# Four output products open at the end, V of the first unit moved, and two rates of a layout clock, in a kernel of two attentions

## The chip, the core and the metric

The kernel runs on one core of a Trainium2 chip. The metric is the time of one execution on the device in microseconds (us), as the median of several runs. The profile is of one execution, taken by the hardware profiler; the last digit of the times of its single instructions is 10 ns.

## What is computed

Two attention layers with their own inputs, both with 2048 positions, width 1024 and 32 heads of 32. Layer A looks back over 8 positions in steps of 2, layer B over 256 positions in a row; their results are put side by side.

```python
qkv = (x @ wqkv).reshape(B, S, 3, H, Dh).transpose(2, 0, 3, 1, 4)
q, k, v = qkv
# A: keys at pos - 2*i for i in 0..7, masked where negative
# B: keys at pos - i for i in 0..255, masked where negative
p = softmax(where(mask, (q @ k.T) * Dh ** -0.5, -1e9))
o = (p @ v).transpose(0, 2, 1, 3).reshape(B, S, D) @ wo
out = concatenate([A, B], axis=-1)
```

## The kernel before

**Units and groups.** The work is cut into eight units of 512 positions (`UNITS`, line 833): units 0 to 3 are layer B (called dense here: scores of up to 384 columns), units 4 to 7 layer A, whose even and odd positions are taken apart so that its window is 8 neighbours (scores of 136 columns). Each unit has eight groups of four heads. With 64 groups in all, group 8u + s is group s of unit u.

**Three-part products.** Each operand of the big products is split into a high part (a cast to fp32r) and a low part (the original less the high part). A product is then three matmuls per step of 128 (`TERMS`: high by high, high by low, low by high). Making the parts is the work of `Stream.parts` (line 126): the cast is done by VectorE (DVE, L129), the subtraction by DVE (L137) or GpSimd (POOL, L134), whichever the layout clock holds to be free earlier. A weight of 128 x 1024 gives one w tile (three buffers); a piece of x gives two x tiles of half its size (ten buffers, `NX`). Raw pieces arrive by DMA in three buffers, so the load of item i + 3 can only start when item i has been split. The first eight loads are issued by ScalarE (ACT), all later ones by POOL (L103).

**Per unit.** For each group: q and k (L363, 24 matmuls of 512 columns each), copied out by ACT (L314) and DVE (L318) and restacked by DMAs that SyncE (SP) issues (L328). V comes in four parts of two groups each (L415, 256 columns), after the q and k of the groups that `V_SLOTS` names. The four parts of the previous unit's attention output are multiplied by `wo` (L455) in eight output products, placed by `O_SLOTS`. Each of these is a chain of eight steps, one for each group, so its last step needs the last group's output.

**Attention of one group.** Sixteen first scores (L614) go to banks of the score ring (four PSUM banks); DVE takes their row maximum with the mask (L619), ACT exponentiates and sums (L624). When all sixteen are done: a logarithm (L637), three small DVE instructions (L642 to L645), a transpose on PE (L653), a copy by DVE (L657) and a DMA back into the q tile (L660). Only then can the second scores run (L509 for the window, L696 for dense), whose exponentials (L514, L701) are masked by DVE or POOL (L524, L520, L682, L685) and multiplied by V (L548, L741). The group's output is copied out in a high part by ACT (L577) and a low part by DVE (L581).

**What sets the order.** Nothing is scheduled by the chip beyond each engine's own queue. While it builds the program, the kernel keeps a layout clock (`Clock`, line 33): it holds estimated times at which each engine and queue becomes free. A loop (line 803) picks from four lists (row transposes, second scores, first scores, big products) the item whose estimated ready time is earliest and emits it; follow-up work on other engines is emitted when the clock passes its time. So a changed rate in the clock alters no instruction but can alter the order of all of them, and which engine does a split or a mask. The clock doesn't model the single output buffer (`NST = 1`): `copy_out` (line 377) chooses between ACT and DVE by when they are free.

**The end.** The eight products of the last unit follow everything else. `TAIL = 2` of them run their first seven steps before the last group's output is there (lines 789 to 797), in two of the three accumulator banks of the big products. Each finished product is copied to the output buffer (L379 by ACT or L382 by DVE) and stored by a DMA that ACT issues (L470).

Of the kernel before, what the change touches and what calls it, by code (L numbers as in the profile page):

```python
# [14 lines left out]
P = 128  # L15
NG = 8
NK = 8
# [6 lines left out]
VPARTS = ((0,2),(2,2),(4,2),(6,2))  # L24
V_SLOTS = {0: 0, 1: 1, 5: 2, 7: 3}
O_SLOTS = {2: (0, 1), 3: (2, 3), 4: (4, 5), 5: (6, 7)}
NX, NST = 10, 1
TAIL, LAND, XAT = 2, 0.45, 1
C1, C3, CG, CV = 0.114, 0.2, 0.231, 0.243
TERMS = ((0, 0), (0, 1), (1, 0))  # L30

# [1 line left out]
class Clock:  # L33
# [26 lines left out]

    def fetch(self, dur, *ready):

        t = max(self.use("pool", 1.0, *ready) + 0.6, self.free["loads"])
        self.free["loads"] = t + dur + 0.5 * max(0.0, min(2 * dur, self.free["copies"] - t))
        return self.free["loads"] + LAND

# [20 lines left out]
class Stream:  # L87
# [19 lines left out]
    def split_to(self, n):  # L107
        while self.split < min(n, len(self.items)):
            i = self.split
            self.load_to(i + 1)  # L110
            raw, t0 = self.raw.pop(i)
            if self.items[i][0] == "x":
                self.tiles[i], self.ready[i] = [], []
                for h in range(2):
                    t = self.xpool.tile([P, 2, S], F32R, tag="x", name="x")
                    self.ready[i].append(self.parts(t, raw[:, h * S:(h + 1) * S], t0))
                    self.tiles[i].append(t)
            else:
                t = self.wpool.tile([P, 2, 1024], F32R, tag="w", name="w")
                self.ready[i] = self.parts(t, raw, t0)  # L120
                self.tiles[i] = t
            self.split += 1
            end = self.ready[i] if self.items[i][0] != "x" else max(self.ready[i])
            self.ck.defer(end, lambda n=i + NRAW + 1: self.load_to(n))

    def parts(self, t, raw, t0):
# [20 lines left out]
def kernel(ctx, tc, xs, wqk, wv, wo, outs, units):  # L147


    nc = tc.nc  # L150
    U = len(units)
# [15 lines left out]
    ck = Clock()  # L167


    plan = []  # L170
    for u in range(U):
        for s in range(NG):
            if u and s in O_SLOTS:
                plan += [("o", u - 1, n) for n in O_SLOTS[s]]
            plan.append(("qk", u, s))
            if s in V_SLOTS:
                plan.append(("v", u, V_SLOTS[s]))
        if u + 1 < U:
            plan.append(("x", u + 1))
    plan += [("o", U - 1, n) for n in range(NG)]  # L180
    items, where = [], {}

    def item(key, kind, ap):
        where[key] = len(items)
        items.append((kind, ap))

    def unit_x(u, *gs):
        for g in gs or range(4):
            item(("x", u, g), "x", xs[u][:, 2 * g:2 * g + 2, :])
# [5 lines left out]
    for p in plan:  # L195
        ly = units[p[1]][0]
        if p[0] == "o":
            item(p, "w", wo[ly, p[2]])
        elif p[0] == "v":
            s0, n = VPARTS[p[2]]  # L200
            for g in range(n):
                if n == 2:
                    item(p + (g,), "w", wv[ly, s0 + g])
                else:
                    w4 = wv[ly, s0 + g // 2:s0 + g // 2 + 3:2, :, g % 2 * 512:g % 2 * 512 + 512]
                    item(p + (g,), "w", w4.rearrange("t p c -> p t c"))
        elif p[0] == "qk":
            for t in range(2):
                if p + (t,) not in where:
                    item(p + (t,), "w", wqk[ly, 2 * p[2] + t])  # L210
        else:
            if NG - 1 in V_SLOTS:
                item(("qk", p[1], 0, 0), "w", wqk[units[p[1]][0], 0])
                unit_x(p[1])
            else:
                unit_x(p[1], 0)
                item(("qk", p[1], 0, 0), "w", wqk[units[p[1]][0], 0])
                unit_x(p[1], 1, 2, 3)
    st = Stream(nc, ck, raws, wpool, xpool, items)
# [42 lines left out]
    xt, xready, ot = {}, {}, {}  # L262
    done, waiting = {}, {}
# [22 lines left out]
    rg, rs, ro = Ring(psg, 7 - NS, "g"), Ring(pss, NS, "s"), Ring(pso, 1, "o")  # L286
# [7 lines left out]
    def latest(*ts):  # L294
        return None if any(t is None for t in ts) else max(ts)
# [81 lines left out]
    def copy_out(dst, ps, bank, ring):  # L377
        if max(ck.free["act"], ck.now) + 0.48 <= max(ck.free["dve"], ck.now) + 0.6:
            nc.scalar.copy(dst, ps)  # L379
            e = ck.use("act", 0.48, ck.now + ck.SEM)  # L380
        else:
            nc.vector.tensor_copy(dst, ps)  # L382
            e = ck.use("dve", 0.6, ck.now + ck.SEM)
        ring.give(bank, e)
        return e
# [52 lines left out]
    def o_items(u, n):  # L438
        h = {}

        def ready(k):
            if (u * NG + k) not in done["ot"]:
                return None
            if k == 0:
                st.split_to(where["o", u, n] + 1)
                h["r"] = st.ready[where["o", u, n]]
                return latest(rg.when(), h["r"], done["ot"][u * NG])
            return done["ot"][u * NG + k]

        def run(k):  # L450
            if k == 0:
                h["ps"], h["b"] = rg.take()
                h["w"], _ = st.get(where["o", u, n])
            for i, (a, b) in enumerate(TERMS):
                nc.tensor.matmul(h["ps"], h["w"][:, a, k * P:(k + 1) * P], ot[u, k][:, b, :],  # L455
                                 start=(k == 0 and i == 0), stop=(k == NK - 1 and i == 2))
            if k == 3 and (u < U - 1 or n != TAIL - 1):
                st.split_to(where["o", u, n] + 2)

        def after(k):  # L460
            if k == NK - 1:
                done["out"][u, n] = True
                for f in list(stores.values()):
                    f()
                o = stp.tile([P, S], F32, tag="ost", name="ost")
                e = copy_out(o, h["ps"], h["b"], rg)

                def store():
                    if stores.pop((u, n), None):
                        nc.scalar.dma_start(outs[u, n], o)  # L470
                        ck.load(0.8, e)

                stores[u, n] = store
                ck.defer(e, store)

        return [(lambda k=k: ready(k), lambda k=k: run(k), 3 * CG, lambda k=k: after(k)) for k in range(NK)]

    def x_items(u):
# [110 lines left out]
    def attention(u, s):  # L589
# [5 lines left out]
        v = vbuf[vp]  # L595
        h = {"left": 16, "rows": None}
        one, two = [], []

        def first(b, j):
            if "nm" not in h:  # L600
                h["nm"] = small.tile([P, 16], F32, tag="nm", name="nm")
                h["sm"] = small.tile([P, 16], F32, tag="sm", name="sm")
            if dense:
                full, mask = 384, cst["mask_d"]
                cut = 0 if has_halo else max(0, 256 - P * b)
            else:
                full, mask = 136, cst["mask_w"]
                cut = 8 if (b == 0 and not has_halo) else 0
            n = full - cut
            c1 = 256 + P * b + P  # L610
            c0 = c1 - n
            i = j * 4 + b
            ps, bank = rs.take()
            nc.tensor.matmul(ps[:, :n], q[0:96, j, b * P:(b + 1) * P], kk[0:96, j, c0:c1],  # L614
                             start=True, stop=True)
            nm, sm = h["nm"][:, i:i + 1], h["sm"][:, i:i + 1]

            def top():
                nc.vector.tensor_tensor_reduce(ps[:, :n], ps[:, :n], mask[:, cut:full], scale=-1.0, scalar=BIG,  # L619
                                               op0=ALU.add, op1=ALU.min, accum_out=nm)  # L620
                e = ck.use("dve", (n + 80) / 960, ck.now)

                def total():
                    nc.scalar.activation(ps[:, :n], ps[:, :n], AF.Exp, bias=nm, scale=-1.0, accum_out=sm)  # L624
                    e2 = ck.use("act", (n + 61) / 1200 + 0.19, e)
                    rs.give(bank, e2)
                    h["left"] -= 1
                    if h["left"] == 0:
                        ck.defer(e2, log_sum)

                ck.defer(e - 0.1, total)

            return top
# [131 lines left out]
    for u in range(U):  # L765
        for s in range(NG):
            a, b = attention(u, s)
# [21 lines left out]
    n = TAIL  # L789
# [13 lines left out]
    while True:  # L803
# [3 lines left out]
        for name, seq in seqs.items():  # L807
# [3 lines left out]
            t = seq[pos[name]].ready()  # L811
# [4 lines left out]
        if ck.later and (best is None or ck.later[0][0] < best[0]):  # L816
            t = ck.later[0][0]
# [3 lines left out]
        t, name = best  # L821
# [52 lines left out]
```

## Time and profile before

| | us |
|---|---|
| median of 3 runs | 1974.42 |
| lowest and highest | 1971.13, 1975.38 |
| the profiled execution | 1973.82 |
| its span, first to last instruction | 1972.1 |
| PE without work, in all, first matmul's 8.05 included | 43.9 |
| mean granted PE clock | 0.987 |

A busy PE is not PE at its peak: matmuls are pipelined, and a run of them is priced by the distance from start to start. Lines of the timeline give start, length, engine, line, operation, output and input tiles, count, and in brackets the idle time of the engine ahead of it with what ended it. Lines of a table of stretches give the stretch, its length, the busy time of PE, PEld (weight loads), DVE, ACT and POOL with instruction counts, then the granted PE clock, the DMA share and GB/s. A line of waits gives who waited for what, the total, how often, and the longest.

### The profile page before, as it was taken

The page shows a single profiled execution, that of the slowest core. Times are in us where ns is not written, and L with a number is a line of the kernel's source. Part 1 is how long each engine was busy: PE and PEld are TensorE (multiplying, and loading weights), DVE is VectorE, ACT ScalarE, POOL GpSimd, SP SyncE. Part 2 cuts the span into 40 slices and gives each one's busy share as a digit, 9 for nine tenths or more (in the row PEclk, how much of TensorE's full clock was granted, in tenths as well). Part 3 has the DMA queues.
Part 4 walks back from the last instruction along what each step waited for, and adds up shares of the span by engine and source line. Part 5 has one row for each costly group of instructions (what it writes and reads, how often), then busy time and mean ns, then how long its engine had stood idle before and what let it go on. Part 6 is the DMA issues. An engine that isn't in the chain of part 4 may idle for free.

```text
span 1972.1 us, 36479 instructions
## 1 busy us (share of the span) xinstructions
PE 1924.7 (98%) x12608; PEld 1619.8 (82%) x12608; DVE 1295.7 (66%) x3762; ACT 957.5 (49%) x3137; POOL 708.7 (36%) x923
## 2 busy tenths in 40 slices
PE   7999999999999999999999999999999999999998
PEld 6878887888877878788878888978888788888886
DVE  5687776678665786567865657655666557666653
ACT  3565554475654656555563344423534334434441
POOL 4334343444433434443443323233332333233221
PEclk9999999999999999999999999999989999999998
DMA  5555546455546465345645647455553565556442
GB/s 176 150 139 153 160 124 178 132 153 157 152 136 174 121 189 149 117 140 148 177 119 146 173 139 196 128 149 170 149 163 116 174 177 162 141 146 172 136 126 75
DMA packets 136502, 294.92 MB, mean 150 GB/s; under 512 B 14464, under 2 KB 42112, under 8 KB 136320
## 3 DMA queue, kind: packets, MB, share of 16 engines
q1 hardware_dynamic: 85632, 124.82, 26.1%
q0 software_dynamic: 40320, 146.82, 22.9%
q10 hardware_dynamic: 10368, 20.98, 2.9%
q8 instruction: 100, 1.64, 0.4%
q14 instruction: 82, 0.67, 0.1%
HBM read 163.58 MB, written 27.26 MB: 97 GB/s over the span
## 4 chain that ended last, share of the span: by engine, by line
PE 84%; DVE 7%; DMA 6%; ACT 2%; issue 1%; SPq 0%; POOL 0%; DVEq 0%; ACTq 0%; POOLq 0%
PE g L363 31%; PE g L455 16%; PE g L415 16%; PE s L614 7%; PE s L696 5%; PE o L741 4%; PE s L509 3%; DMA qst<-rt 3%; PE o L548 2%; DMA kst<-nat 1%; DMA raw<-xs 1%; DVE x L137 1%; DVE w L129 1%; ACT s L624 1%; DVE w L137 1%
## 5 line engine op out<-in xcount | busy, mean ns | idle before, releaser
L363 PE MATMUL g<-x,w 128*128 128x512 f32 x3072 | 801.9, 401 | 8.6 <-DVE w L129 8.0
L134 POOL TENSOR_TENSOR w<-raw,w 128x512 fp32r<-128x512 f32 x225 | 392.5, 1745 | 897.2 <-PE s L614 285.7
L363 PEld LDWEIGHTS g<-x,w 128*128 128x128 f32 x3072 | 562.0, 191 | 110.9 <-DVE w L129 8.4
L624 ACT ACTIVATE s<-s,nm 128x384 f32<-128x384 f32 (+3 forms) x1024 | 452.3, 443 | 231.0 <-DVE nm L619 227.1
L415 PE MATMUL g<-w,x 128*128 128x256 f32 x3072 | 413.3, 285 | 0.0
L415 PEld LDWEIGHTS g<-w,x 128*128 128x128 f32 x3072 | 392.7, 191 | 1.9 <-issue 0.6
L455 PE MATMUL g<-ot,w 128*128 128x512 f32 x1536 | 384.2, 397 | 3.6 <-DVE w L129 2.9
L455 PEld LDWEIGHTS g<-ot,w 128*128 128x128 f32 x1536 | 283.8, 190 | 58.1 <-DVE w L129 3.6
L619 DVE CUSTOM_DVE_ANT_0 s<-s,mask_d 128x384 f32<-128x384 f32 (+2 forms) x512 | 262.0, 556 | 72.9 <-PE s L614 71.5
L614 PE MATMUL s<-kst,qst 96*128 96x384 f32 (+3 forms) x1024 | 238.7, 303 | 16.2 <-ACT s L624 7.1
L701 ACT ACTIVATE pbuf<-s 128x384 f32<-128x384 f32 (+2 forms) x480 | 197.1, 507 | 85.5 <-PE s L696 81.8
L614 PEld LDWEIGHTS s<-kst,qst 96*128 96x128 f32 x1024 | 181.3, 192 | 60.5 <-ACT s L624 18.1
L624 ACT ACTIVATION_READ_ACCUMULATOR s<-s,nm 128x1 f32 x1024 | 210.2, 205 | 0.0
L619 DVE CUSTOM_DVE_ANT_0 s<-s,mask_w 128x136 f32<-128x136 f32 (+1 forms) x512 | 142.4, 322 | 98.4 <-PE s L614 96.8
L129 DVE CAST w<-raw 128x1024 fp32r<-128x1024 f32 x256 | 199.9, 781 | 9.4 <-PE g L455 9.4
L137 DVE TENSOR_TENSOR w<-raw,w 128x512 fp32r<-128x512 f32 x287 | 197.2, 696 | 8.8
L682 POOL TENSOR_SCALAR_AFFINE_SELECT pbuf<-pbuf 128x128 f32<-128x128 f32 (+1 forms) x383 | 147.9, 404 | 150.1 <-ACT pbuf L701 143.5
L314 ACT ACTIVATE nat<-g 128x512 fp32r<-128x512 f32 x128 | 76.6, 598 | 255.2 <-PE g L363 247.8
L318 DVE SCALAR_TENSOR_TENSOR nat<-g,nat 128x512 fp32r<-128x512 f32 x128 | 88.3, 690 | 145.5 <-ACT nat L314 134.9
L524 DVE TENSOR_TENSOR pbuf<-pbuf,keep_w 128x272 f32<-128x272 f32 (+1 forms) x224 | 116.9, 566 | 61.5 <-ACT pbuf L514 60.6
L619 DVE DVE_READ_ACCUMULATOR2_ANT nm<- 128x1 f32 x1024 | 144.3, 141 | 0.0
L696 PEld LDWEIGHTS s<-qst,kst 98*128 98x128 f32 x704 | 106.2, 189 | 37.8 <-PE o L741 10.0
(48 smaller groups left out, 1227.3 us busy)
## 6 DMA issues: line engine op xcount, KB each, us to landing
raw<-wqk POOLq DMA_DIRECT2D x126, 512.0 KB, 3.7
qst<-nat SPq DMA_DIRECT2D x192, 256.0 KB
kst<-nat SPq DMA_DIRECT2D x192, 256.0 KB
raw<-wo POOLq DMA_DIRECT2D x64, 512.0 KB, 3.7
raw<-wv POOLq DMA_DIRECT2D x62, 512.0 KB, 4.5
outs<-ost ACTq DMA_DIRECT2D x64, 256.0 KB
raw<-xs POOLq DMA_DIRECT2D x28, 512.0 KB, 4.8
halo<-nat SPq DMA_DIRECT2D x40, 256.0 KB
```

Of the source, the lines that this page charges most:

```text
L129: nc.vector.tensor_copy(t[:, 0, :], raw)
L134: nc.gpsimd.tensor_tensor(o, a, b, op=ALU.subtract)
L137: nc.vector.tensor_tensor(o, a, b, op=ALU.subtract)
L363: nc.tensor.matmul(h["ps"], h["w"][:, a, k * P:(k + 1) * P], xt[u][k][:, b, :], start=(k == 0 and i == 0), stop=(k == NK - 1 and i == 2))
L415: nc.tensor.matmul(ps, xt[u][k][:, a, p0:p0 + P], h["w"][:, c, k % kw], start=(k == 0 and i == 0 and r == 0), stop=(k == NK - 1 and i == 2 ...
L455: nc.tensor.matmul(h["ps"], h["w"][:, a, k * P:(k + 1) * P], ot[u, k][:, b, :], start=(k == 0 and i == 0), stop=(k == NK - 1 and i == 2))
L614: nc.tensor.matmul(ps[:, :n], q[0:96, j, b * P:(b + 1) * P], kk[0:96, j, c0:c1], start=True, stop=True)
L619: nc.vector.tensor_tensor_reduce(ps[:, :n], ps[:, :n], mask[:, cut:full], scale=-1.0, scalar=BIG, op0=ALU.add, op1=ALU.min, accum_out=nm)
L624: nc.scalar.activation(ps[:, :n], ps[:, :n], AF.Exp, bias=nm, scale=-1.0, accum_out=sm)
L682: nc.gpsimd.affine_select(w, w, pattern=[[0, m], [step, n]], compare_op=ALU.is_ge, fill=0.0, base=base, channel_multiplier=chan)
L696: nc.tensor.matmul(ps[:, i * n:(i + 1) * n], kk[0:98, j, 256 + kb * P:256 + (kb + 1) * P], q[0:98, j, q0:q0 + n], start=True, stop=True)
L701: nc.scalar.activation(w, ps[:, :pack * n].rearrange("p (j n) -> p j n", j=pack), AF.Exp)
```

## The change

Three things are changed. At the end, four products instead of two run their first seven steps ahead of the last group's output; the fourth has its accumulator in a bank of the score ring, and the weights of products 3 to 7 of the last unit are split into x tiles (two halves) instead of w tiles, at new points (k = 3 and k = 5 of earlier products). In unit 0, V parts 1 and 2 come after groups 2 and 4 instead of 1 and 5. In the layout clock, a load's issue on POOL counts 0.6 us instead of 1.0, with 0.9 instead of 0.6 until it starts, and the row maximum on DVE counts (n + 110) / 960 us instead of (n + 80) / 960.

```diff
+V0_SLOTS = {0:0,2:1,4:2,7:3}
-TAIL, LAND, XAT = 2, 0.45, 1
+TAIL, LAND, XAT = 4, 0.45, 1
...
-        t = max(self.use("pool", 1.0, *ready) + 0.6, self.free["loads"])
+        t = max(self.use("pool", 0.6, *ready) + 0.9, self.free["loads"])
...
-            if self.items[i][0] == "x":
+            if self.items[i][0] != "w":
...
-            if s in V_SLOTS:
-                plan.append(("v", u, V_SLOTS[s]))
+            vs = V_SLOTS if u else V0_SLOTS
+            if s in vs:
+                plan.append(("v", u, vs[s]))
...
-            item(p, "w", wo[ly, p[2]])
+            item(p, "w" if p[1] < U - 1 or p[2] < 3 else "xw", wo[ly, p[2]])
...
+        last = u == U - 1
+        ring = rs if last and n == 3 else rg
+
         def ready(k):
...
             if k == 0:
                 st.split_to(where["o", u, n] + 1)
-                h["r"] = st.ready[where["o", u, n]]
-                return latest(rg.when(), h["r"], done["ot"][u * NG])
-            return done["ot"][u * NG + k]
+                r = st.ready[where["o", u, n]]
+                h["r"] = r if isinstance(r, list) else [r, r]
+                return latest(ring.when(), h["r"][0], done["ot"][u * NG])
+            return max(done["ot"][u * NG + k], h["r"][k // 4])
 
         def run(k):
             if k == 0:
-                h["ps"], h["b"] = rg.take()
-                h["w"], _ = st.get(where["o", u, n])
+                h["ps"], h["b"] = ring.take()
+                w, _ = st.get(where["o", u, n])
+                h["w"] = [(w[i // 4], i % 4 * P) if isinstance(w, list) else (w, i * P) for i in range(NK)]
+            w, c = h["w"][k]
             for i, (a, b) in enumerate(TERMS):
-                nc.tensor.matmul(h["ps"], h["w"][:, a, k * P:(k + 1) * P], ot[u, k][:, b, :],
+                nc.tensor.matmul(h["ps"], w[:, a, c:c + P], ot[u, k][:, b, :],
                                  start=(k == 0 and i == 0), stop=(k == NK - 1 and i == 2))
-            if k == 3 and (u < U - 1 or n != TAIL - 1):
-                st.split_to(where["o", u, n] + 2)
+            if k == 3 and (not last or n == 0 or n > 2):
+                st.split_to(where["o", u, n] + (3 if last and n == 0 else 2))
+            if k == 5 and last and n in (1, 2):
+                st.split_to(where["o", u, n] + 3)
...
-                e = copy_out(o, h["ps"], h["b"], rg)
+                e = copy_out(o, h["ps"], h["b"], ring)
...
-                e = ck.use("dve", (n + 80) / 960, ck.now)
+                e = ck.use("dve", (n + 110) / 960, ck.now)
```

More of the change, by code (lines that the diff above doesn't have):

```diff
@@ L122, in split_to @@
             self.split += 1
-            end = self.ready[i] if self.items[i][0] != "x" else max(self.ready[i])
+            end = self.ready[i] if self.items[i][0] == "w" else max(self.ready[i])
             self.ck.defer(end, lambda n=i + NRAW + 1: self.load_to(n))
```

## The prediction, made before the changed kernel was run

> **What bounds the kernel now.** The page first: TensorE (PE) is busy 98% of the span, the next engine, VectorE (DVE), 66%. The multiplications are the same before and after, so only time in which PE stands, or runs at a lower clock, can be won.
>
> ```profile
> span 1972.1 us, 36479 instructions
> PE 1924.7 (98%) x12608; PEld 1619.8 (82%) x12608; DVE 1295.7 (66%) x3762; ACT 957.5 (49%) x3137; POOL 708.7 (36%) x923
> ```
>
> Then the waits of PE, longest total first: 8.0 us is the start (first weights), and no kind of wait in the middle reaches 8 us in total.
>
> ```profile
> PE g L363 <- DVE w L129: 8.0, 1, 8.0
> PE s L614 <- ACT s L624: 7.1, 8, 1.2
> PE s L509 <- DMA qst<-rt: 6.7, 10, 1.8
> ...
> PE g L455 <- DVE w L129: 2.9, 1, 2.9
> ```
>
> Third, the timeline of the last 60 us. There the reader sees three holes close together: PE waits 1.36 us for the row of sums to come back by DMA, 0.70 us for the last group's output, and 2.85 us for the weights of product 2. Those weights are late because DVE, before splitting them, waits to copy product 1 into the one output buffer, which product 0's store still holds from 1929.67 to 1931.83 (2.16 us).
>
> ```profile
> 1918.07 0.67 SPq L660 DMA_DIRECT2D qst<-rt  x1
> 1920.49 3.64 PEld L509 LDWEIGHTS s<-qst,kst 98*128 98x128 f32 x20 [1.76 <-issue]
> 1920.52 3.80 PE L509 MATMUL s<-qst,kst 98*128 98x8 f32 x20 [1.36 <-DMA qst<-rt]
> ...
> 1927.09 3.23 PE L455 MATMUL g<-ot,w 128*128 128x512 f32 x6 [0.70 <-ACT ot L577]
> ...
> 1929.08 0.59 ACT L379 COPY ost<-g 128x512 f32<-128x512 f32 x1 [2.04 <-PE g L455]
> ...
> 1931.83 0.69 DVE L382 COPY ost<-g 128x512 f32<-128x512 f32 x1 [4.06 <-DMA outs<-ost]
> ...
> 1933.17 35.35 PE L455 MATMUL g<-ot,w 128*128 128x512 f32 x144 [2.85 <-DVE w L129]
> ```
>
> Fourth, a table of stretches of 4 us and one of 10 us; the column after POOL is the granted PE clock. The holes cost more than their length: the clock is halved for most of 1921 to 1938. Adding (1 - clock) x 4 us over the five rows gives 8.5 us. Earlier, one hole of 2.01 us (at 31) is followed by a 10 us stretch at 0.83, so 1.7 us lost, which is 3.4 us at half clock.
>
> ```profile
> 30.00:40.00 10.00, 7.99 (x53) 7.82 (x53) 5.25 (x22) 3.44 (x15) 2.29 (x2) 0.83 0.52 162
> ...
> 1920.00:1924.00 4.00, 3.48 (x20) 3.51 (x20) 2.15 (x6) 2.57 (x7) 0.23 (x1) 0.66 0.00 0
> 1924.00:1928.00 4.00, 3.29 (x44) 1.90 (x44) 1.77 (x3) 1.18 (x2) 0.00 (x0) 0.50 0.00 0
> 1928.00:1932.00 4.00, 2.32 (x5) 1.31 (x5) 0.17 (x1) 0.59 (x1) 0.00 (x0) 0.50 0.17 66
> 1932.00:1936.00 4.00, 2.83 (x7) 2.20 (x8) 3.93 (x5) 0.00 (x0) 2.35 (x2) 0.50 0.17 66
> 1936.00:1940.00 4.00, 4.00 (x14) 3.20 (x13) 2.77 (x5) 0.00 (x0) 1.05 (x2) 0.71 0.74 238
> ```
>
> **Part 1, the tail.** Prices: 48 product matmuls in a row take 10.88 us in the chain, so 0.227 each; half an x tile split on DVE (cast, then subtract) 1.06 us (1446.10, 1446.56, 1447.16); score matmuls 0.126 each (8 in 1.01 us at 1903.78); the 40 value matmuls 1.19 us (1908.48).
>
> In the changed kernel's order PE has, after the transpose of the row sums (L653, at 1917.51 now): 21 product matmuls instead of 6; 12 of the 20 score matmuls, 3 products, the other 8, 3 products, 15 of product 3 (its accumulator lies in a score bank); the 40 value matmuls; 6 of product 3; then the last step of all four products (12), and 96 for products 4 to 7. Up to L653 the amount is unchanged (36). I follow it from 1917.5:
> - DVE now splits product 3's two halves ahead of the copy of the row sums: 1916.2 + 2.1 = 1918.4 instead of 1917.77. The DMA took 2.47 us from the copy's end to PE, so it lands at 1921.1. PE has 21 x 0.227 = 4.8 us of products, until 1922.3. The wait of 1.36 us goes; the scores start 1.8 us later.
> - DVE splits product 4 (2.1 us) between the first and the other masks (0.42 each, last 0.69): masks end near 1929.0 where they ended at 1925.7. PE meanwhile has 20 x 0.126 + 21 x 0.227 = 7.3 us, until 1929.7, so these splits cost nothing; without that cover the 2.1 us would show. Values end at 1930.9; 6 products until 1932.2; high and low copy of the output (0.59 + 0.69, as at 1926.45) until 1932.3. The 0.70 us goes.
> - Next late: the output buffer. Product 0 is copied by ACT from about 1933.0 to 1933.6; products 1, 2, 3 are all copied by DVE, each after the store ahead: 3 x (2.16 + 0.69) gives 1942.1. Queued behind them on DVE are the splits of products 5 to 7, so PE gets product 5 at about 1942.65. Its 12 + 24 matmuls last only until 1932.3 + 36 x 0.227 = 1940.4: a new wait of 2.2 us. The four stores stand in ACT's queue ahead of product 4's copy, whose bank is needed only by product 7.
> - I charge the clock as after the 2.01 us hole: 1.7 us. Products 5 to 7 are 72 x 0.227 = 16.3 us; end of PE 1960.7, against 1968.5. **-7.8 us.** Both ends: no clock loss -9.5; 17 us at half clock as now (8.5 us) -1.0.
>
> The Trainium skill says in "TensorE: Matmul & The Clock Gate", section "Why this matters for your kernels", that gaps up to about 3 us between bursts do not lower the clock. The 0.83 row behind the 2.01 us hole speaks against it, and so does 213 us below. By that rule the tail would gain 9.5 us.
>
> **Part 2, V of the first unit.** Group 6 of unit 0 loses 2.2 us now (0.92 before the transpose at 211.42, 0.97 at 213.13, and small ones), and then 1.7 us of clock (the stretch 210 to 220 is at 0.83). DVE and ACT are overfull there. V's third part now comes one group earlier, and the order then has 4.1 us of PE work from the group's last score to the transpose and 3.9 from there to its second scores; where it is 4.1 and 3.9 now (group 2) PE waits 0.2. So -3.6. Groups 2, 3 and 5 lose 1.2 us together now and get 4.7 to 6.0 us ahead of the transpose; I take -1.0. Against it, group 1 has 2.3 us of PE work between transpose and second scores where it had 3.4 and waited 0.68: +1.1, and one chance in three of a clock loss (of three waits of 1.25 us at 469, 729 and 987 the last alone was followed by one), +0.6. **-2.9 us**; ends -5 and +2.
>
> **Part 3, the layout clock's rates.** They issue nothing; they change the order everywhere: 8145 of PE's 11330 matmuls keep their place in sequence. The new DVE rate is the truer: (384 + 110) / 960 = 0.515 us, and two L619 of 384 columns start 0.52 apart (464.15, 464.67); the old gave 0.483. The 0.6 for a load on POOL is also what its issues take (0.57). 52 more masks go to POOL, which is 36% busy: nothing. But truer rates need not give fewer waits, so I went through the 64 groups by PE work ahead of the transpose and of the second scores. In units 1 to 3 groups 14 and 22 have 2.0 us of products ahead of the transpose; groups that waited there needed 4.6 to 5.0 from the last score, so I allow 2.4 each instead of 1.6, and a third of 1.7 of clock: +2.7 for both. Groups 16 and 24 fall from 7.1 to 3.6 us: +0.5 each. Groups 10 and 18 gain 0.6 each. In units 4 to 7 the order is nearly the old one; group 46 has 4.1 us for the returning row instead of 3.4, and may lose one half-clock stretch less: -1.5; groups 36 and 52 have 3.0 instead of 3.7: +1. The sum is +2.0, to be read as an estimate: ends -6 (most waits of units 1 to 3 gone) and +16 (rival 2).
>
> **Sum.** -7.8 - 2.9 + 2.0 = -8.7. The profiled execution took 1973.82 us (span 1972.1 and 1.7 around it), 0.6 below the median of 1974.42. 1973.8 - 8.7 = 1965.1; I say **1965.3 us**.
>
> **Rivals.**
> 1. *The output buffer keeps PE cold.* The new wait stands where the old one stood, and half clock lasts as long as before: tail -1.0, time 1972. For: 17 us at half now, behind three holes. Against: two of the three are filled. 0.08.
> 2. *The row-sum chain is late after the new order* (slower). It decides if groups 14, 16, 22, 24 of the dense units get their log-sums after a weight split and a nat copy that stand ahead on DVE and ACT: at 5.0 us needed, 14 and 22 wait 2.9 and lose two half-clock stretches (3.4), less the 1.6 they wait now, so +4.7 each; 16 and 24 wait 1.4 + 1.7 less 0.1, +3.0 each; groups 9, 17 and 25, with 4.1 us, wait 0.9 each: together 18.1 instead of the 3.7 charged. Sum -8.7 + 14.4 = +5.7: 1979.5. Slower begins where these seven cost over 12.4. For: the 2.0 us. Against: such groups wait 1.6 now. 0.10; half of that price, 0.09, within 0.2%.
> 3. *Short holes do not lower the clock*, as that page has it: 1.7 + 0.6 + 1.1 less, time 1962. Against: 31 and 213 us. 0.08.
> 4. *The change doesn't do what it says*: excluded by the order for the tail (63 + 21 products stand ahead of the end), so no chance of its own.
>
> **How the numbers follow.** Forecast 0.65 (1959 to 1970), rival 1 0.08, rival 2 0.10, its half-way form 0.09, rival 3 0.08. Range 1958 to 1972: part 2 and part 3 at good ends below, rival 1 above. About 0.2%, 3.9 us, is what a measurement here tells from no change. Faster: forecast, rival 3 and half of rival 1 (whose 1972 may fall on either side of 1970.5), 0.77; within: the other half of rival 1 and the half-way form, 0.13; slower: rival 2, 0.10.
>
> **What would show it.** In the last 60 us: no PE wait ahead of the second scores and none on the last output; a PE wait of about 2.2 us on an x split behind three ost copies by DVE, 2.9 us apart; half clock 3.4 us instead of 17. At 205 to 220 us: no stretch below 1.0. Wrong if the wait for product 5 is over 4 us, or if units 1 to 3 show new stretches of half clock behind L653's wait.

## The result, and the profile after

The changed kernel took 1987.49 us (median, 1978.82 to 1990.89) beside 1972.77 of the kernel before on the same chip: 1.0069 of it [1.004, 1.0097]. By this ratio it is slower by 13.6 us, where 8.7 were to be won. In the page's first lines PE's work has hardly changed, and the span has grown:

```profile
span 1988.2 us, 36474 instructions
...
PE 1929.4 (97%) x12608; PEld 1622.1 (82%) x12608; DVE 1288.9 (65%) x3713; ACT 955.8 (48%) x3135; POOL 741.3 (37%) x979
```

The waits of PE, after the change (lines from L314 on have moved by 2 to 10: L614 is now L624, L619 L629, L653 L663, L509 L519, L455 L463). Columns as before: total, how often, longest.

```profile
PE s L624 <- DMA kst<-nat: 15.2, 10, 3.4
PE s L663 <- DVE hl L655: 8.5, 14, 2.4
PE g L365 <- DVE w L130: 8.2, 2, 7.9
PE s L519 <- DMA qst<-rt: 6.7, 15, 1.0
...
```

The first two lines are the news. Before the change the same two kinds stood at 5.7 and 3.4 us; they have grown by 14.6 us together.

```profile
PE s L614 <- DMA kst<-nat: 5.7, 5, 2.0
PE s L653 <- DVE hl L645: 3.4, 10, 0.5
```

The accounts of the profiled executions, in us. Half-clock loss is the sum of (1 - granted clock) x time up to PE's end; rest is the end less idle and loss. The rows with an e in brackets are experiments below.

| kernel | last row transpose | PE's end | PE idle | half-clock loss | rest |
|---|---|---|---|---|---|
| before | 1917.5 | 1968.5 | 43.9 | 25.6 | 1899 |
| after | 1940.6 | 1984.6 | 55.2 | 29.0 | 1900 |
| tail alone (e1) | 1916.0 | 1954.9 | 40.7 | 11.9 | 1902 |
| tail, new rate of the row maximum (e2) | 1936.9 | 1980.7 | 55.9 | 23.9 | 1901 |
| whole change, a stack's DMA counted 1.3 (e9) | 1909.6 | 1952.8 | 39.0 | 8.5 | 1905 |
| tail, short stacks (e17) | 1912.7 | 1953.7 | 34.7 | 20.5 | 1899 |
| as e2, short stacks (e18) | 1900.2 | 1944.2 | 38.7 | 3.4 | 1902 |

So after loses 23.1 us up to the last row transpose, 20.1 of them by the transpose of group 31, the end of the dense units, and wins 7.0 behind it. (e1 is not to be compared by this column: 15 of its products, 3.4 us, stand ahead of the last transpose that stand behind it in after.) The tail did what was forecast; PE's timeline there:

```profile
1940.64 0.22 PE L663 MATMUL s<-ident,hl 128*32 128x128 f32 x1
1940.69 5.02 PE L463 MATMUL g<-ot,w 128*128 128x512 f32 x21
1946.13 1.53 PE L519 MATMUL s<-qst,kst 98*128 98x8 f32 x12 [0.41 <-DMA qst<-rt]
...
1958.71 5.60 PE L463 MATMUL g<-ot,x 128*128 128x512 f32 x24
1966.41 2.89 PE L463 MATMUL g<-ot,x 128*128 128x512 f32 x6 [2.10 <-DVE x L130]
```

The wait for the last output is gone, and product 5 waits 2.10 us (2.2 forecast). On DVE the three copies into the one output buffer start 2.86 and 2.85 us apart, as priced:

```profile
1959.62 0.69 DVE L384 COPY ost<-g 128x512 f32<-128x512 f32 x1 [3.71 <-DMA outs<-ost]
1962.48 0.69 DVE L384 COPY ost<-g 128x512 f32<-128x512 f32 x1 [2.17 <-DMA outs<-ost]
1965.33 0.69 DVE L384 COPY ost<-s 128x512 f32<-128x512 f32 x1 [2.16 <-DMA outs<-ost]
```

The table of stretches (the clock is the column after POOL) holds one 3.4 us window of half clock here, 1.7 us lost, and 6.8 us of half clock where V was moved, from 215 on, where none was forecast:

```profile
1964.00:1968.00 4.00, 1.90 (x6) 1.23 (x5) 2.60 (x5) 0.00 (x0) 0.00 (x0) 0.81 0.35 131
1968.00:1972.00 4.00, 4.00 (x16) 3.18 (x15) 3.86 (x9) 0.58 (x1) 0.00 (x0) 0.76 0.17 66
...
205.00:210.00 5.00, 4.34 (x31) 2.55 (x29) 3.08 (x10) 1.94 (x6) 0.77 (x2) 1.00 1.02 255
210.00:215.00 5.00, 2.62 (x9) 1.53 (x9) 1.41 (x3) 0.60 (x1) 2.36 (x2) 1.00 1.05 258
215.00:220.00 5.00, 4.01 (x12) 3.46 (x13) 2.96 (x12) 1.65 (x7) 1.72 (x1) 0.54 0.37 137
```

How the dense units lose shows at the end of one. Group 31's K stack, kernel before, from its timeline: issued at 969.23, first scores at 984.61, and PE has had other work all the way.

```profile
969.23 1.92 SPq L328 DMA_DIRECT2D kst<-nat  x3
...
984.61 0.51 PE L614 MATMUL s<-kst,qst 96*128 96x384 f32 x2
```

The same place after:

```profile
993.95 1.92 SPq L330 DMA_DIRECT2D kst<-nat  x3
...
1005.37 1.62 PE L624 MATMUL s<-kst,qst 96*128 96x384 f32 x4 [3.38 <-DMA kst<-nat]
```

Between the first issue and the scores lay 14.1 us of big products before (matmuls priced at 0.227 and 0.12) and 5.0 after; for groups 15, 23 and 7 it is 14.2, 14.2 and 12.0 before, 5.2, 6.1 and 5.0 after. Where PE waits for the stack, 9.3 us (group 7) and 10.1 us (group 31) pass from its last issue to the scores; the layout clock counts three DMAs at 0.95, so 2.9. While group 7's stack is under way the DMA engines are full: 1.02 and 1.05 in the column after the clock, in the rows of 205 to 215.

A late stack also holds the row sums. After, at 738, ACT's copy of the next q (L316) waits 2.15 us because stack DMAs still read its `nat` buffer; behind it in ACT's queue stand the last exponential of the group ahead (L634) and its logarithm (L647), and so PE's transpose (L663) waits 2.36:

```profile
738.36 0.60 ACT L316 ACTIVATE nat<-g 128x512 fp32r<-128x512 f32 x1 [2.15 <-DMA qst<-nat]
738.85 0.55 ACT L634 ACTIVATE s<-s,nm 128x384 f32<-128x384 f32 x1
...
739.55 0.21 ACT L647 ACTIVATE ln<-sm 128x16 f32<-128x16 f32 x1
...
740.53 0.22 PE L663 MATMUL s<-ident,hl 128*32 128x128 f32 x1 [2.36 <-DVE hl L655]
```

### The profile page after: what moved, and what is told of

It is laid out like the page before. It is cut to its first block, busy times and chain, and to the rows that moved or that the text cites. A ratio compares the mean times of both kernels' runs of the same rounds, so it can differ in the third digit from the quotient of the medians.

```text
span 1988.2 us, 36474 instructions
## 1 busy us (share of the span) xinstructions
PE 1929.4 (97%) x12608; PEld 1622.1 (82%) x12608; DVE 1288.9 (65%) x3713; ACT 955.8 (48%) x3135; POOL 741.3 (37%) x979
## 4 chain that ended last, share of the span: by engine, by line
PE 79%; DMA 10%; DVE 7%; issue 2%; ACT 2%; POOL 0%; SPq 0%; DVEq 0%; ACTq 0%; POOLq 0%
PE g L365 29%; PE g L417 15%; PE g L463 15%; PE s L624 7%; PE s L706 5%; DMA qst<-rt 4%; PE o L751 4%; PE s L519 3%; DMA kst<-nat 3%; PE o L558 2%; DMA qst<-nat 1%; DVE x L138 1%; DMA raw<-xs 1%; DVE w L130 1%; DVE x L130 1%
## 5 line engine op out<-in xcount | busy, mean ns | idle before, releaser
L135 POOL TENSOR_TENSOR w<-raw,w 128x512 fp32r<-128x512 f32 x229 | 399.1, 1743 | 909.5 <-issue 282.3
L634 ACT ACTIVATE s<-s,nm 128x384 f32<-128x384 f32 (+3 forms) x1024 | 452.2, 443 | 265.5 <-DVE nm L629 258.7
L463 PE MATMUL g<-ot,w 128*128 128x512 f32 x1416 | 358.1, 395 | 0.0
L629 DVE CUSTOM_DVE_ANT_0 s<-s,mask_d 128x384 f32<-128x384 f32 (+2 forms) x512 | 262.2, 555 | 99.8 <-PE s L624 98.8
L463 PEld LDWEIGHTS g<-ot,w 128*128 128x128 f32 x1416 | 259.5, 189 | 46.7 <-issue 0.2
L624 PE MATMUL s<-kst,qst 96*128 96x384 f32 (+3 forms) x1024 | 234.3, 303 | 24.0 <-DMA kst<-nat 15.2
L624 PEld LDWEIGHTS s<-kst,qst 96*128 96x128 f32 x1024 | 180.3, 193 | 66.2 <-issue 29.3
L692 POOL TENSOR_SCALAR_AFFINE_SELECT pbuf<-pbuf 128x128 f32<-128x128 f32 (+1 forms) x435 | 173.4, 420 | 140.3 <-ACT pbuf L711 135.8
L634 ACT ACTIVATION_READ_ACCUMULATOR s<-s,nm 128x1 f32 x1024 | 210.3, 205 | 0.0
L629 DVE CUSTOM_DVE_ANT_0 s<-s,mask_w 128x136 f32<-128x136 f32 (+1 forms) x512 | 142.0, 322 | 104.2 <-PE s L624 102.8
L316 ACT ACTIVATE nat<-g 128x512 fp32r<-128x512 f32 x128 | 76.5, 598 | 266.6 <-PE g L365 252.4
L138 DVE TENSOR_TENSOR w<-raw,w 128x512 fp32r<-128x512 f32 x273 | 188.9, 699 | 8.6
L130 DVE CAST w<-raw 128x1024 fp32r<-128x1024 f32 x251 | 193.3, 770 | 0.0
L629 DVE DVE_READ_ACCUMULATOR2_ANT nm<- 128x1 f32 x1024 | 143.4, 140 | 0.0
```

The costliest lines, as they stand in the source:

```text
L130: nc.vector.tensor_copy(t[:, 0, :], raw)
L135: nc.gpsimd.tensor_tensor(o, a, b, op=ALU.subtract)
L138: nc.vector.tensor_tensor(o, a, b, op=ALU.subtract)
L463: nc.tensor.matmul(h["ps"], w[:, a, c:c + P], ot[u, k][:, b, :], start=(k == 0 and i == 0), stop=(k == NK - 1 and i == 2))
L692: nc.gpsimd.affine_select(w, w, pattern=[[0, m], [step, n]], compare_op=ALU.is_ge, fill=0.0, base=base, channel_multiplier=chan)
```

## The experiments

**Theory 1**: the loss comes from the stacks, which in the new orders land late against the first scores and copies that the layout sets right behind them. **Theory 2** stands for its rivals: other chains of the order are late, or any new order is a draw that mostly comes out worse than the old. In the expectations of e1 to e4 the theories are named by the part of the change instead: 1 is the rate of the row maximum, 2 the moved V, 3 the load's rate. Ratios are to the kernel before on the same chip; single runs of one kernel lie up to 10.5 us from its median, so only medians of several count. Where an expectation has -8.5 for e1 and 20.5 for the rate of the row maximum, these are differences of medians; the ratios give -6.7 and 18.7.

All but the two kernels with the whole change (e9, e16) hold product 3's first step back until the last second scores are placed (with the old rate of the row maximum it would take a score bank that these need). With the change's own rates this leaves PE's order as it is.

```diff
+            if k == 0 and ring is rs and pos["2"] < len(twos) - 1:
+                return None
```

**Each part.** From the changed kernel, V's slots and both rates are put back; then one at a time is brought in.

```diff
-V0_SLOTS = {0:0,2:1,4:2,7:3}
+V0_SLOTS = {0: 0, 1: 1, 5: 2, 7: 3}
...
-        t = max(self.use("pool", 0.6, *ready) + 0.9, self.free["loads"])
+        t = max(self.use("pool", 1.0, *ready) + 0.6, self.free["loads"])
...
-                e = ck.use("dve", (n + 110) / 960, ck.now)
+                e = ck.use("dve", (n + 80) / 960, ck.now)
```

e1 has all three put back; e2 keeps n + 110, e3 keeps V0_SLOTS, e4 keeps 0.6 and 0.9.

> The end alone: V slots and both rates as before, four products open at the end. One condition is added in all four kernels here: product 3 may take its score bank only when all second scores are placed (with the change's own rates this gives the changed kernel's order matmul by matmul). Up to PE's matmul 11114 of 11328 the order is that of before. All theories: the end gains what the two traces show, 23.1 us later at the last row transpose but 16.1 later at the last matmul, so -7.0 us (-5 to -9). If it gains under 3 us, the gain seen in the changed kernel belongs to the late arrival of its last unit and not to the four products.

Measured 0.9966 [0.9941, 0.9991], so -6.7 us: the tail is won.

> The end and the new rate of the row maximum; V slots and the load's rate as before. Theory 1 (the DVE rate brings the loss, by orders in which the last group of a dense unit gets its stacks late): the stretches of units 1 to 3 lose 20.3 us more than before less what belongs to the V slots; with the end's -7, between +5 and +13 us against before, with PE waits of 2 us and more near the ends of dense units. Theory 2 (the moved V of unit 0 brings it): -7. Theory 3 (the load's rate): -7.

1.0061 [1.004, 1.0081]: this rate alone costs 18.7 us over e1 (1.0061 - 0.9966, times 1971), and is inside the range that was given for it.

> The end and the moved V of unit 0; both rates as before. Theory 1: -7 and what unit 0 itself gives, between -3 and +5, so -10 to -2. Theory 2 (the V slots bring most of the loss, in unit 0 and by what they leave to units 1 to 3): +5 to +15. Theory 3 (the load's rate): -7.

0.9984 [0.9966, 1.0003]: 3.5 us worse than e1, with overlapping intervals. Group 7's K stack is issued with 5 us of products left ahead of its scores, instead of 12.

> The end and the load's rate; V slots and the row maximum's rate as before. PE's order is that of before up to matmul 2915 (in unit 2). Theories 1 and 2: -7 within 3. Theory 3 (loads planned earlier share the queues with the stacks, so that the K stack comes late): +5 to +15 with longer waits of first scores on the K stack than before's 5.7 us.

1.0014 [0.9994, 1.0033]: 9.5 us worse than e1. No theory had this, and late stacks are not the cause: groups 15, 23 and 31 have 14 us of products ahead of their scores as in e1. The cause is open. The three parts do not add up either: 18.7, 3.5 and 9.5 over e1, where the whole change stands 20.3 over it (1.0069 - 0.9966, times 1972).

**Where the rate acts.** e5 has the new rate in the window units alone (below), e6 in the dense units alone.

```diff
-                e = ck.use("dve", (n + 110) / 960, ck.now)
+                e = ck.use("dve", (n + (80 if dense else 110)) / 960, ck.now)
```

> The end as changed, and the new rate of the row maximum for the window units (4 to 7) alone; PE's order is that of before up to matmul 5784. The end alone measured -8.5 us against before, end and rate +12, so the rate costs 20.5. Theory 1 (the cost is made at the ends of the dense units, where the last group's K stack is issued 12 us of products later and 5 to 6 us of products ahead of its first scores instead of 14): under 6 us of the 20.5 are here, so -9 to -3. Theory 2 (any new order costs, wherever it is new, because the old one is a favourable draw): about half, so -1 to +5.

1.001 [0.9991, 1.0028], a miss of theory 1 and inside theory 2's range: 8.7 us worse than e1.

> The other half: the end, and the new rate for the dense units (0 to 3) alone. Theory 1: 14 us or more of the 20.5, so +6 to +12. Theory 2: -1 to +5. If both halves together cost much less than 20.5, the two interact.

1.0068 [1.0045, 1.0091], 20.1 us worse than e1 and a little above theory 1's range: as much as e2 on its own. The two halves come to 28.8 us where the whole rate costs 18.7; the paragraph on waits and clock below shows why.

**The loads' share.** e2 with x of units 1 to 4 and V's last weights of units 0 to 3 not loaded; these units compute with zeros.

```diff
+            if self.loaded in self.cut:
+                self.nc.gpsimd.memset(raw, 0.0)
+            else:
...
```

> End and new rate for all units, with the same order of PE, but the x of units 1 to 4 and V's last weights of units 0 to 3 are not loaded: POOL fills their raw buffers with zeros instead of issuing the load, so these units compute with zeros. Theory 1a (the stacks of the last groups are late because x and V loads share the DMA queues with them, which makes a stack take 9 to 12 us): the waits at 246, 445 to 480, 738 and 1003 us, 16.6 us in the trace, and their half-clock stretches shrink; at least 8 us under e2_tail_dve. Theory 1b (they are only issued too late, the queues being no matter): within 3 us of e2_tail_dve.

1.0034 [1.002, 1.0049], 5.3 us better than e2, with overlapping intervals and between the bounds of both theories. At the unit ends its four holes are still 1.93, 2.50, 3.76 and 4.12 us, where e2 has 2.36, 2.34, 4.48 and 5.84: the loads that share the DMA engines explain about a quarter by the medians, and PE waits at the same places without them.

**The count of a stack.**

```diff
-                ck.copy(0.55 if dense else 0.35, ck.now)
+                ck.copy(0.75 if dense else 0.5, ck.now)
...
-                        e2 = ck.copy(0.95, e, ck.now)
+                        e2 = ck.copy(1.3, e, ck.now)
```

e8 is this on e2, e9 on the whole change, e10 on e1.

> End and new rate, and in the layout clock a stack DMA counts 1.3 us instead of 0.95 (halo reads 0.75 and 0.5 instead of 0.55 and 0.35); what is computed and issued is the same. Theory 1: the layout now sees stacks arrive later, and places them or their scores better: at least 5 us under e2_tail_dve. Theory 2: another draw, between 4 us under and any amount over e2_tail_dve.

0.9994 [0.9974, 1.0014]: 13.2 us better than e2.

> The whole change, and in the layout clock a stack DMA counts 1.3 us instead of 0.95 (halo reads 0.75 and 0.5). Theory 1 (the changed rates make plans that need the stacks earlier than they come): the 13.2 us between e2 and e8 come off here too, so +15 becomes -3 to +6 against before. Theory 2 (each new order is a draw, the old one favourable): +5 to +25.

0.9949 [0.9927, 0.997]: 24 us better than the change as it came (1.0069), more than theory 1 had, and faster than the kernel before. The kind of wait that led after's list is gone from the head of this one:

```profile
PE g L365 <- DVE w L130: 8.6, 3, 8.0
PE s L663 <- DVE hl L655: 7.1, 13, 1.3
PE s L624 <- ACT s L634: 4.7, 5, 2.1
PE s L706 <- DMA qst<-rt: 4.1, 4, 2.0
```

Waits for the K stack are 1.1 us in all there. Groups 15, 23 and 31 have 6.8, 6.8 and 9.3 us of products ahead of their scores now; group 7 has 2.0, but other work of PE fills the 7.1 us from the last issue to its scores, so products alone do not measure the cover.

> The end alone, old rates and V slots, with the stack DMA at 1.3 us. Theory 1: the waits of first and second scores on DMAs, 7.5 and 5.0 us in the trace of the end alone, and the half-clock stretches of units 5 and 6 shrink, so -12 to -22 against before (the end alone: -8.5). Theory 2: -8.5 and a loss, -5 to +12.

0.9958 [0.9943, 0.9973], a miss: 8.3 us below the kernel before instead of 12 to 22, and no better than e1 within the intervals. To the old rates the longer count brought nothing that can be measured.

**Other rates, a test of chance.** e11 and e12 are e1 with n + 65 and n + 95; e13 is e12, e14 is e4 with the 1.3; e15 is e2 with 1.3 in the dense units alone; e16 is the whole change with 1.6 (halo 0.9 or 0.6).

> The end alone, and the row maximum counted as (n + 65) / 960, which is further from what the chip takes than the old 80. Theory 1 (a slower row maximum in the plan moves second scores behind the next group's first scores, so that stacks are freed late): no such move here, within 5 of the end alone, so -14 to -4 against before. Theory 2 (a draw): 0 to +12.

1.0 [0.9985, 1.0015], 6.7 us worse than e1: theory 1 missed. A smaller rate costs, too. But its reason for expecting nothing, that the stacks stay where they are, did not hold: in this order groups 15, 23 and 31 have 6.8, 6.8 and 9.5 us of products ahead of their scores, where e1 has 14.

> The end alone, and the row maximum counted as (n + 95) / 960, half way to the new rate. Theory 1: a threshold somewhere between 80 and 110; by the plan's order of groups 15, 23 and 31 either near the end alone (-14 to -4) or near e2 (+5 to +15), according to where their K stacks are issued (477 or 489 us of big products done, for group 23). Theory 2: 0 to +12 whichever.

1.0056 [1.0037, 1.0075], with K stacks issued as late as in e2; both theories allow this.

> The tail with a row maximum of (n + 95) / 960 and a stack DMA counted 1.3 us (a halo read 0.75 or 0.5). With 0.95 the same rate gave 1985.2 us, 1.0056 of the kernel before. Theory 1 (the loss comes from stacks that the layout counts as too short): the loss goes, ratio 0.994 to 1.000, at least 11 us under the 1.0056. Theory 2 (any other order of the dense units is a draw, mostly worse than the old one): the three sets that came out well with 1.3 were luck; this one comes out at 1.001 or more.

0.9977 [0.9962, 0.9993]: held, 15.6 us better than e12.

> The tail with the load's new rate alone (0.6 and 0.9) and a stack DMA counted 1.3 us. With 0.95 it gave 1974.5 us, 1.0014. Theory 1: 0.994 to 0.9985. Theory 2: as likely above 1.0014 as below it; over 1.001 speaks for it.

0.9984 [0.9966, 1.0002]: held at its edge, 5.9 us better than e4, with overlapping intervals.

> The tail with a row maximum of (n + 110) / 960 and a stack DMA counted 1.3 us in the dense units alone (0.95 in the window units). With 0.95 everywhere 1.0061, with 1.3 everywhere 0.9994. If the dense units are where the short count does its harm (all of the rate's cost came from them), most of the 13 us comes back: 0.999 to 1.002. If half of the gain lay in the window units, as the profile with 1.3 everywhere shows, 1.0025 to 1.004. Theory 2: no order, 1.000 to 1.008.

1.0048 [1.0031, 1.0064], above both ranges of theory 1, though the interval overlaps the second: only 2.6 of the 13 us came back. By the traces this run joins two known orders: PE's first 6370 matmuls come as in e8, its last 5814 (the window units) as in e2. So the larger part of what 1.3 won lay in the window units, which no expectation had.

> The whole change with a stack DMA counted 1.6 us (a halo read 0.9 or 0.6) instead of 0.95. With 1.3 the whole change gave 0.9949, with 0.95 1.0069. Theory 1: the layout has enough reserve at 1.3, so this stays within 5 us of it: 0.9925 to 0.998. Theory 2: another draw, 0.998 to 1.006.

0.9955 [0.9938, 0.9971]: held. With 0.95 counted everywhere, nine sets of rates and slots gave 0.9966 to 1.0069; with 1.3 or 1.6 everywhere, six gave 0.9949 to 0.9994, no median slower than before. Why one set does better than another within such a row stays open.

**The stacks themselves.** The last pair leaves every order alone: from the third group on, of the three DMAs of a Q or K stack only the first is issued, and the layout clock still counts three. On every engine but SP the instructions are those of e1 and e2.

```diff
-                        nc.sync.dma_start(dst[i:96:3, :, c:c + S].bitcast(F32), hl[:, a, :].bitcast(F32))
+                        if i == 0 or hg < 2:
+                            nc.sync.dma_start(dst[i:96:3, :, c:c + S].bitcast(F32), hl[:, a, :].bitcast(F32))
```

> The tail with the old rates, and of the three DMAs of a stack only the first issued from the third group on (the rows of the two low-order terms keep an earlier group's values, so the output is off in its last places); the layout clock counts all three, so every other engine's order is that of the tail alone (0.9966 of the kernel before). Both theories: 0 to 8 us better than the tail alone, 0.992 to 0.997, as its waits for stacks at the ends of the dense units become shorter.

0.9946 [0.9925, 0.9967]: 3.9 us better than e1, with overlapping intervals.

> The same short stacks in the order with (n + 110) / 960, which with full stacks gave 1.0061. Its distance from the tail alone is 18.7 us with full stacks (1.0061 less 0.9966, of 1971). Theory 1 (this order loses because its first scores and copies stand right behind stacks that land late): with stacks of a third of the bytes and issues the distance from e17 falls to 8 us or less. Theory 2 (the order's other chains, on VectorE and ScalarE, are what costs): the distance stays at 14 us or more. Between the two, both have a share.

0.9935 [0.9919, 0.9952]: 24.8 us better than e2 (1.0061 - 0.9935, times 1970). The distance of the two orders is not 18.7 us any more but -2.2, within the intervals of zero. Theory 2's 14 or more is out: what this order loses hangs on its stacks, though not all of it is waits for them (below). PE's waits in e2:

```profile
PE s L665 <- DVE hl L657: 11.9, 12, 4.5
PE s L626 <- DMA kst<-nat: 11.6, 7, 5.8
```

And in e18, the same order with short stacks (L666 and L627 are the same two lines):

```profile
PE s L666 <- DVE hl L658: 7.5, 12, 2.0
...
PE s L627 <- DMA kst<-nat: 1.9, 1, 1.9
```

The two kinds fall by 14.1 us, the one on the row sums among them, as the chain at 738 has it. The half-clock loss falls from 23.9 to 3.4 us with them (e18's profiled run is the shortest of its six, 5.9 us under their median, so this is at its best). e17's profile has less idle time (34.7 us) but 20.5 of half-clock loss: short holes lower the clock in one order and not in another, and why is open. What makes a stack late, its bytes, its three issues on SP or its place, was not taken apart; short stacks also leave more room on the DMA engines for all other transfers.

**Waits and clock apart.** Every run's span and mean granted clock are on record. Span x (1 - clock) is an estimate of its half-clock loss, and what is left of the span holds the waits. Medians, in us:

| kernel | half-clock loss | span less loss |
|---|---|---|
| before (beside e1 to e4) | 23.6 | 1946.3 |
| after | 27.8 | 1959.2 |
| e1 | 13.7 | 1947.0 |
| e2 | 21.8 | 1960.4 |
| e5 | 21.7 | 1950.2 |
| e6 | 23.8 | 1957.8 |
| e9 | 15.7 | 1946.6 |
| e17 | 18.6 | 1939.1 |
| e18 | 10.7 | 1943.7 |

Single runs of one kernel differ mostly in the first column (e1's ten: 10 to 22), so much of their spread is the clock. (The kernel before has 19.7 to 23.6 and 1945.0 to 1947.0 on the chips used here, so across chips the second column tells differences to about 2 us; e1 and e2 ran on one chip, e17 and e18 on another.) The second column adds up: over e1, e5 costs 3.2 and e6 10.8, together 14.0, and e2 13.4. It is the clock that does not, at 8.0, 10.1 and 8.1. So the halves do not speak for theory 2. PE's last 5814 matmuls come in the same order in e2, e5, e15 and after, and took 887.3, 893.2, 879.6 and 893.8 us in their profiles, with 10.2, 17.1, 5.1 and 15.4 of half-clock loss: the same order, and the clock is the draw. And with short stacks e2's order still stands 4.6 us behind e1's in the second column (1943.7 - 1939.1) where it stood 13.4. Some two thirds of its extra waits go with the stacks; the rest of the way to -2.2 is half-clock loss, which fell in e18 and rose in e17.

## Why the prediction was wrong

- **Part 1, the tail: right.** -7.0 us in the profile (from the last row transpose to PE's end 51.0 before, 44.0 after) and -6.7 by e1, for -7.8. The forecast had most of it from the clock (8.5 lost before, 1.7 after), and so it came: over all runs e1 has 9.9 us less of half-clock loss than before, and 0.7 more of the rest. The wait for product 5 was 2.10 (2.2) and one half-clock window followed it (1.7 charged, 1.7 found); that it followed is in part luck (last section). Only "no PE wait ahead of the second scores" was off, by 0.41 us. Rival 1 is out.
- **Part 2, V of the first unit: wrong, by the medians in sign.** The waits of group 6 did shrink (0.52 ahead of the transpose at 208.89 where it was 0.92; the 0.97 is gone). But with V's parts moved group 7's K stack is issued with 5.0 us of products ahead of its scores: a wait of 3.29 us at 215.99 and two windows of half clock. +3.5 us by e3, with overlapping intervals, for -2.9. The step compared the row-sum chain of group 6 and never the stack of group 7.
- **Part 3, the two rates: the step that failed.** "I went through the 64 groups by PE work ahead of the transpose and of the second scores": that is one of the two loops that close outside PE. The other, from the K stack's issue to the first scores, was not looked at, though the kernel issues a stack only when the output of two groups earlier is done, and the order after shows when that is. The term was +2.0; from e3 to the whole change it is +16.8 (1.0069 - 0.9984, times 1972). Even its bad end, +16, was tied to another mechanism. For the largest part, the rate of the row maximum, the cause is shown: e18 keeps its order, shortens the stacks, and the 18.7 us are gone, by the waits (13.4 to 4.6) and by the clock. Why e4's order loses, and what the last 4.6 are, stays open.
- **Rival 2** had the sign and some of the places (groups 14 and 22 waited 1.77 and 2.36 for the row sums, for 2.4 as allowed), with another cause: behind the nat copy it names stands the stack that still reads the buffer. Groups 16 and 24, charged with 0.5 each, waited 0 and 0.28. What the prediction named as a sign against itself, "if units 1 to 3 show new stretches of half clock behind L653's wait", came true at 478 and 741; those at 448 and 1004 stand behind first scores.
- **"The new DVE rate is the truer"** is so by its row, and still cost 18.7 us: a truer rate for one engine beside a count for the stacks that is too short by a factor of three sets the first scores closer to stacks that are not there.
- **Rival 3**, that short holes do not lower the clock, is out as a rule (below), though not every hole of 2 us lowered it.

## What to carry to other kernels

Where an estimate decides the order, list every loop that leaves the busiest engine and returns to it (here two: row sums, stacks) and measure for each how much work covers it in the old and in the new order; one loop checked is half a forecast. When a rate is corrected, look for the error elsewhere that the old rate made good: the fix that paid here was the count of the stack's DMA (1.0069 to 0.9949 with the whole change). To tell a late transfer from a bad order, keep the order and shrink the transfer. And where the granted clock of every run is on record, take waits and clock apart before two orders are compared: here one order of the window units took 879.6 to 893.8 us, by 5.1 to 17.1 us of half-clock loss.

## What the runs showed of the hardware

Holes of about 2 us were mostly followed by half clock, but not always. In after's table of stretches, holes of 2.00 us (ending at 446.16), 1.77 (477.83) and 2.36 (740.53) stand ahead of these rows, each 1.7 us lost:

```profile
447.00:451.00 4.00, 4.00 (x20) 3.79 (x19) 3.96 (x11) 3.02 (x10) 1.52 (x1) 0.57 0.02 8
...
478.00:482.00 4.00, 4.00 (x13) 3.16 (x13) 1.60 (x4) 0.00 (x0) 2.29 (x2) 0.57 0.78 258
...
741.00:745.00 4.00, 3.30 (x9) 2.07 (x7) 1.37 (x3) 0.00 (x0) 2.29 (x2) 0.57 0.77 245
```

The wait for product 5, 2.10 to 2.47 us long, comes near the end in all 19 profiles with four open products. A window of half clock began within 2 us behind or beside it in 15 of them and in none of e1, e6, e10 and e15. e1's row with its hole, from 1935.87 to 1937.97; the row after it is at 1.00 too:

```profile
1936.00:1940.00 4.00, 2.03 (x8) 1.39 (x9) 3.05 (x6) 0.27 (x1) 0.00 (x0) 1.00 0.25 93
```

So the length of a hole alone does not decide it; what else does was not tested. The Trainium skill, in "TensorE: Matmul & The Clock Gate", section "Why this matters for your kernels", advises against idle gaps over about 3 us between bursts of matmuls. Keeping under that was not enough in after's rows above.

The other surprise is the stack's latency: beside loads, 9.3 and 10.1 us passed after, and 11.7 in e2, from the last of a stack's three issues to the scores that waited for it.
